# Three VectorE instructions fewer in the prologue of a one-token attention and MLP block

## The chip, the cores and the metric

The kernel runs on one core of a Trainium2 chip. The metric is the device time of one execution in microseconds. The kernel before took 191.74 us, the median of three runs (191.66 to 191.85).

The core's engines run side by side and meet at semaphores: TensorE (PE in the profile) multiplies matrices, VectorE (DVE) does elementwise work, reductions and 32x32 transposes, ScalarE (ACT) does functions such as exp and gelu, GpSimd (POOL) does general work, and SyncE (SP) issues most of the loads. Sixteen DMA engines move data between memory and the on-chip buffers. SBUF is the on-chip memory with 128 partitions, PSUM the accumulators that TensorE writes.

## The reference

One token passes through a layer norm, attention against a cache of 16384 keys and values with 32 query heads on 8 key heads, an output projection, and an MLP. In short:

```python
def _A_ref(x, k_cache, v_cache, wq, wo):
    q = (x @ wq).reshape(B, Sq, Hq, Dh).transpose(0, 2, 1, 3)
    k = jnp.repeat(k_cache, rep, axis=1)        # 8 key heads -> 32
    v = jnp.repeat(v_cache, rep, axis=1)
    scores = jnp.einsum("bhqd,bhkd->bhqk", q, k) * (Dh ** -0.5)
    p = _softmax(scores, axis=-1)
    o = jnp.einsum("bhqk,bhkd->bhqd", p, v)
    return o.transpose(0, 2, 1, 3).reshape(B, Sq, Hq * Dh) @ wo
...
x = A_x                                          # [1, 1, 512]
h = x + _A_ref(_layernorm(x), A_k_cache, A_v_cache, A_wq, A_wo)
h2 = h + _B_ref(_layernorm(h), B_w1, B_w2, B_w3, B_w4)
```

In `_B_ref` the shifted branch (`w1`, `w2`) is zero for a single token, since every shift moves the one row out; what is left is `gelu(layernorm(x) @ w3) @ w4` beside the residuals. The inputs are bf16: each of the two caches is 33.5 MB, wq and wo are 4.2 MB each, w3 and w4 1.8 MB each. Together that is the 79.17 MB that the profile counts as read.

## The kernel before, in words

The kernel is written as a list of operations with named tiles; a helper class turns reads and writes of the same name into semaphore waits. On each engine the instructions run in the order in which the program lists them. All large loads go through one queue, issued by SP in program order; a load waits until its target buffer is free.

There are three large buffers: `kb` (keys, two halves), `vb` (values) and `kt` (transposed keys). `wq` is loaded into `vb`, `wo` into the first half of `kb`, and `w3` and `w4` into the second half of `kb`, when these are free.

1. *Prologue* (lines 325 to 394). The token is loaded as four rows of 128 (`x4`). VectorE sets `mean4` and clears `ident_f`; GpSimd writes ones on its diagonal (line 332), which makes an fp32 unit matrix. Line 337 casts its top left 4x4 corner to bf16 (`ident`), line 338 spreads each of the four columns 32 times (`quarter`, 4 x 4 x 32). A matmul with `quarter` as weights (line 340) puts each of the four rows of the token on 32 partitions. A chain of small VectorE instructions computes the layer norm and ends in `xn` (line 346).
   Behind it VectorE sets constants: `nscale` (351), columns 2 and 3 of a scratch tile (352), two fields of zeros `zo` and `zd` of 128 x 224 fp32 (354, 355), and then masks made from `ident_f` (359 to 368). Two copies (370) put 32 columns of a mask into the middle of `zo` and `zd`; sliding a 128-column window over such a field places one pair's result in its own 32 rows (lines 436 and 464). GpSimd meanwhile clears `qb` and `pt` (356, 357). ScalarE loads its table for exp with a dummy instruction (353).
   Then TensorE multiplies `xn` with `wq` (381), and VectorE transposes and scatters the queries into `qb` (385, 391).
2. *Four pairs of key heads.* For each pair: VectorE transposes the keys in eight pieces for each half (400), TensorE computes scores (408), a short chain finds the maximum and takes exp on ScalarE (419 to 430), VectorE transposes the probabilities (434), TensorE multiplies with the values (447), and VectorE and TensorE gather the result (458 to 464). A key buffer is reloaded after its transposes, the value buffer after the products.
3. *End.* Output projection (506), second layer norm, the two MLP products (540, 568), sums (572, 574), and two small stores.

`spin` (line 263) issues matmuls whose results nobody reads.

Of the kernel before, what the change touches and what calls it, by code (L numbers as in the profile page):

```python
# [6 lines left out]
FP32 = mybir.dt.float32  # L7
BF16 = mybir.dt.bfloat16
# [124 lines left out]
def bass_sequential_preLN__gqa_block_cached__mixer_s_mlp__decode_kernel(  # L133
# [13 lines left out]
    with ExitStack() as ctx:  # L147
        sb = lambda name, shape, dt: ctx.enter_context(nc.sbuf_tensor(name, shape, dt))
# [15 lines left out]
        x4 = sb("x4", [4, 128], BF16)  # L164
        mean4 = sb("mean4", [128, 128], FP32)
        ident_f = sb("ident_f", [128, 128], FP32)
        ident = sb("ident", [4, 4], BF16)
        quarter = sb("quarter", [4, 4, 32], BF16)
        row32 = sb("row32", [128, 32], FP32)
        maskdd = sb("maskdd", [128, 4], FP32)  # L170
        maskgh = sb("maskgh", [128, 2, REP], FP32)
        rowgh = sb("rowgh", [128, 2, REP], FP32)
        rowc = sb("rowc", [128, 4], FP32)
        zo = sb("zo", [128, 224], FP32)
        zd = sb("zd", [128, 224], FP32)
        nscale = sb("nscale", [1, 128], FP32)
        scr = sb("scr", [128, 4], FP32)
        st = [sb(f"st{i}", [128, 16], FP32) for i in range(2)]
# [66 lines left out]
        def dve(fn, r=(), w=(), bank=()):  # L245
            return P.op("DVE", fn, r, w, bank)

        def act(fn, r=(), w=(), bank=()):
            return P.op("ACT", fn, r, w, bank)

        def pool(fn, r=(), w=(), bank=()):
            return P.op("POOL", fn, r, w, bank)

        def pe(fn, r=(), w=(), bank=()):
            return P.op("PE", fn, r, w, bank)

        def piece(cuts, m):
            return [lo <= m < hi for lo, hi in cuts].index(True)
# [49 lines left out]
        def inverse_root(i, n, by):  # L308
# [25 lines left out]
                                               channel_multiplier=1), r=["ident_f"], w=["ident_f"])  # L334


        dve(lambda e: e.tensor_copy(ident[:, :], ident_f[0:4, 0:4]), r=["ident_f"], w=["ident"])  # L337
        dve(lambda e: e.tensor_copy(quarter[:, :, :], ident[:, :].unsqueeze(2).to_broadcast([4, 4, 32])),  # L338
            r=["ident"], w=["quarter"])
        pe(lambda e: e.matmul(O_ps[0][:, 0:128], quarter[:, :, :].rearrange("p q u -> p (q u)"), x4[:, :],  # L340
                              start=True, stop=True), r=["quarter", "x4"], w=[("O", 0)], bank=[("O", 0)])
        row_sums(0, O_ps[0], ("O", 0))
# [5 lines left out]
            r=["hT", (("st", 0), 0), (("st", 0), 6)], w=["xn"])  # L348


        dve(lambda e: e.memset(nscale[:, :], -SCALE), w=["nscale"])
        dve(lambda e: e.memset(scr[:, 2:4], 0.0), w=["scr2"])
        act(lambda e: e.activation(scr[0:1, 0:1], mean4[0:1, 0:1], ACTF.Exp), r=["mean4"], w=["scr"])
        dve(lambda e: e.memset(zo[:, :], 0.0), w=["zo"])
        dve(lambda e: e.memset(zd[:, :], 0.0), w=["zd"])
        pool(lambda e: e.memset(qb[:, :, :, :], 0.0), w=["qb"])
        pool(lambda e: e.memset(pt[:, :, :, :, :], 0.0), w=["pt"])

# [1 line left out]
            r=["ident_f"], w=["row32"])  # L360
        dve(lambda e: e.tensor_reduce(maskdd[:, :], ident_f[:, :].rearrange("p (n d) -> p d n", d=4), AX.X, ALU.add),
            r=["ident_f"], w=["maskdd"])
# [14 lines left out]
        for j, (row, key) in enumerate(rows):  # L377
# [6 lines left out]
            for b in range(2):  # L384
# [3 lines left out]
                    r=[key], w=["qcol"], bank=[key])  # L388
# [103 lines left out]
        for n, (lo, hi) in enumerate(W4):  # L492
# [7 lines left out]
            r=["o_m"], w=["o_f"])  # L500
# [3 lines left out]
        for r_ in range(32):  # L504
# [3 lines left out]
               r=["o_b", ("r", 0, piece(WO, r_))], w=[("O", 0)], bank=[("O", 0)])  # L508
# [3 lines left out]
           r=["quarter", "x4"], w=[hkey], bank=[hkey])  # L512
# [7 lines left out]
        for q in range(4):  # L520
            pe(lambda e, q=q: e.matmul(h_ps[32 * q:32 * q + 32, 0:128], copies(row32[:, 0:1], 32),
                                       osum[:, q * 128:(q + 1) * 128], start=False, stop=True, skip_group_check=True),
               r=["osum", "row32"], w=[hkey], bank=[hkey])
# [3 lines left out]
        for i in range(2):  # L527
# [5 lines left out]
            r=["hT", (S, 0)], w=["hc"])  # L533
        act(lambda e: e.activation(hr2[64:128, :], h2_ps[64:128, 0:256], ACTF.Identity, bias=0.0, scale=1.0),
            r=["h2"], w=["hr2"], bank=["h2"])


        for k in range(NCH):
            for q in range(4):
                pe(lambda e, k=k, q=q: e.matmul(s_ps[32 * q:32 * q + 32, 0, 0:FQ], hc[:, k, :],  # L540
                                                w3_sb[:, k, q * FQ:(q + 1) * FQ], start=(k == 0), stop=(k == NCH - 1)),
                   r=["hc", ("r", 1, piece(W3, k))], w=[("s", 0)], bank=[("s", 0)])
# [7 lines left out]
        for n in range(2):  # L550
# [9 lines left out]
            r=["hr2", "xs2"], w=["xsum"])  # L560

        turns = {m: m % 2 if m < W4[0][1] else 0 for m in range(NHC)}
        for m in range(NHC):
# [3 lines left out]
            for o in range(2):  # L567
# [3 lines left out]
                   r=[("hcol", 2 * m // NHC), ("r", 1, 2 + piece(W4, m))], w=[key], bank=[("B" if t else "mn")])  # L571
        dve(lambda e: e.tensor_tensor(part[:, :], xsum[64:128, :], B_ps[64:128, 0:256], ALU.add),
            r=["B", "xsum"], w=["part"], bank=["B"])
        dve(lambda e: e.tensor_tensor(fin[:, :], part[:, :], n_ps[0:64, 0:256], ALU.add),  # L574
            r=["n", "part"], w=["fin"], bank=["mn"])
        for o, by in enumerate(("SP", "ACT")):
            P.op(by, lambda e, o=o: e.dma_start(out[0, 0:1, 256 * o:256 * o + 256], fin[32 * o:32 * o + 1, :]),
                 r=["fin"], w=[("out", o)], dma=f"out{o}")
# [32 lines left out]
```

## Time and profile before

| what | us |
|---|---|
| median of three runs | 191.74 |
| the profiled execution | 191.69 |
| its span, first to last instruction | 190.2 |
| TensorE busy in it | 116.7 (61%) |
| VectorE busy in it | 116.0 (61%) |
| ScalarE, GpSimd busy | 9.4, 7.0 |
| read from memory | 79.17 MB, 416 GB/s over the span |

In the rows that follow, `out<-in` names tiles, `x8` counts instructions, `L338` is a line of the kernel, and a bracket tells how long the engine had been idle before and what released it (`[5.81 <-DMA ...]`). `SPq` is SP's queue of DMA issues. Times are microseconds from the start of the span, unless a column is said to be in nanoseconds. In groups of instructions the numbers behind the bar are busy time, mean nanoseconds of one, and idle time before.

### The profile page before, as it was taken

How to read it: one execution, taken by the hardware profiler on the slowest of the kernel's cores; microseconds unless marked ns; L12 is line 12 of the kernel's file. 1: busy time of each engine (PE TensorE's matmuls, PEld its weight loads, DVE VectorE, ACT ScalarE, POOL GpSimd, SP SyncE). 2: the span in 40 equal slices, each digit the busy share in tenths (PEclk: the TensorE clock that was granted, in tenths of full speed). 3: DMA queues.
4: the chain of work that ended last, by engine and by line, in shares of the span. 5: the costliest groups of instructions: out<-in, count | busy, mean ns of one | idle time of the engine just before them, and what ended most of it. 6: DMA issues, size and time to landing. Idle time of an engine off the chain costs nothing.

```text
span 190.2 us, 1684 instructions
## 1 busy us (share of the span) xinstructions
PE 116.7 (61%) x700; PEld 43.7 (23%) x703; DVE 116.0 (61%) x179; ACT 9.4 (5%) x16; POOL 7.0 (4%) x15
## 2 busy tenths in 40 slices
PE   0128099893084004999447799935739896598673
PEld 0113034221031001422123222212213222233231
DVE  7756397983402007999452999844259897514274
ACT  3000000002000000000110000020000000500011
POOL 7100000000000000000000000000000000000032
PEclk9999858998559655899958999995796999669999
DMA  6999999999999999997999998999999999989992
GB/s 221 441 441 441 441 441 443 441 441 431 441 441 441 441 427 441 441 441 341 441 420 441 496 455 386 403 407 407 441 441 441 469 444 413 441 379 393 428 410 76
DMA packets 2610, 79.26 MB, mean 417 GB/s; under 512 B 298, under 2 KB 428, under 8 KB 556
## 3 DMA queue, kind: packets, MB, share of 16 engines
q1 hardware_dynamic: 2594, 79.17, 97.1%
q8 instruction: 5, 0.08, 0.2%
q14 instruction: 1, 0.01, 0.0%
q10 hardware_dynamic: 10, 0.00, 0.0%
HBM read 79.17 MB, written 0.00 MB: 416 GB/s over the span
## 4 chain that ended last, share of the span: by engine, by line
DMA 61%; DVE 31%; PE 4%; issue 1%; SPq 1%; ACT 1%; ACTq 0%
DMA kb<-in_A_k_cache_dram 47%; DVE kt L400 28%; DMA kb<-in_B_w_dram 15%; PE O_ps L447 3%; DVE pt L434 1%; SPq L226 1%; DVE mx L419 1%; ACT p_sb L430 1%; DVE od L461 1%; PE s_ps L408 1%; PE mn_ps L568 0%; DVE fin L574 0%; PE mn_ps L424 0%; PE mn_ps L420 0%; DVE od L458 0%
## 5 line engine op out<-in xcount | busy, mean ns | idle before, releaser
L408 PE MATMUL s_ps<-kt,qb 128*128 128x512 bf16 x256 | 69.3, 408 | 27.1 <-DVE kt L400 24.0
L400 DVE STREAM_TRANSPOSE kt<-kb 128x1024 int32<-128x1024 int32 x64 | 72.8, 1206 | 19.3 <-DMA kb<-in_A_k_cache_dram 19.3
L408 PEld LDWEIGHTS s_ps<-kt,qb 128*128 128x128 bf16 x256 | 22.4, 102 | 73.1 <-DVE kt L400 50.1
L447 PE MATMUL O_ps<-vb,pt 128*32 128x512 bf16 x256 | 20.0, 481 | 9.4 <-DMA vb<-in_A_v_cache_dram 7.4
L458 DVE TENSOR_SCALAR od<-O_ps,rowc 128x128 f32<-128x128 f32 x4 | 1.4, 351 | 26.3 <-PE O_ps L447 26.3
L434 DVE STREAM_TRANSPOSE pt<-p_sb 64x1024 bf16<-64x1024 bf16 x8 | 9.9, 1239 | 5.4 <-ACT p_sb L430 5.3
L447 PEld LDWEIGHTS O_ps<-vb,pt 128*32 128x32 bf16 x256 | 8.2, 117 | 20.3 <-issue 8.8
L430 ACT ACTIVATE p_sb<-s_ps,bias 128x1024 bf16<-128x1024 f32 x4 | 4.5, 1113 | 156.6 <-DVE nmh L426 156.6
L263 PE MATMUL O_ps<-kt,qb 128*128 128x512 bf16 x26 | 8.8, 478 | 0.6 <-issue 0.6
L419 DVE TENSOR_REDUCE mx<-s_ps 128x1 f32<-128x1024 f32 x4 | 4.9, 1224 | 4.5 <-PE s_ps L408 4.5
L381 PE MATMUL O_ps<-vb,xn 128*64 128x512 bf16 x16 | 3.2, 574 | 5.8 <-DMA vb<-in_A_wq_dram 5.8
L315 POOL TENSOR_SCALAR st<-st 128x1 f32<-128x1 f32 x1 | 0.2, 244 | 177.7 <-DVE st L300 177.7
L436 PE MATMUL A_ps<-acc,zd 128*128 128x1 f32 x8 | 2.1, 337 | 6.3 <-ACT p_sb L430 6.3
L464 PE MATMUL A_ps<-od,zo 128*128 128x128 f32 x8 | 2.0, 326 | 5.5 <-DVE od L461 5.5
L420 PE MATMUL mn_ps<-ident_f,mx 128*1 128x128 f32 x8 | 1.5, 271 | 5.3 <-DVE mx L419 5.3
L461 DVE SCALAR_TENSOR_TENSOR od<-O_ps,rowc,od 128x128 f32<-128x128 f32 x12 | 4.2, 351 | 0.4
L263 PEld LDWEIGHTS O_ps<-kt,qb 128*128 128x128 bf16 x29 | 3.1, 121 | 4.8 <-issue 3.7
L337 DVE CAST ident<-ident_f 4x4 bf16<-4x4 f32 x1 | 3.8, 3849 | 0.6 <-POOL ident_f L332 0.6
L340 PE MATMUL O_ps<-x,quarter 4*128 4x128 bf16 x1 | 0.3, 281 | 5.8 <-DVE quarter L338 5.8
L385 DVE STREAM_TRANSPOSE qcol<-O_ps 128x256 f32<-128x256 f32 x4 | 1.6, 428 | 3.4 <-PE O_ps L381 3.4
L436 PEld LDWEIGHTS A_ps<-acc,zd 128*128 128x128 f32 x8 | 1.8, 281 | 6.6 <-ACT p_sb L430 6.6
L506 PE MATMUL O_ps<-kb,o_b 128*32 128x512 bf16 x32 | 2.1, 381 | 1.6 <-DMA kb<-in_A_wo_dram 1.6
(90 smaller groups left out, 49.3 us busy)
## 6 DMA issues: line engine op xcount, KB each, us to landing
kb<-in_A_k_cache_dram SPq DMA_DIRECT2D x6, 4096.0 KB, 24.0
vb<-in_A_wq_dram SPq DMA_DIRECT2D x1, 4096.0 KB, 12.4
kb<-in_A_wo_dram SPq DMA_DIRECT2D x1, 3072.0 KB, 27.2
kb<-in_B_w_dram SPq DMA_DIRECT2D x1, 1792.0 KB, 24.4
kb<-in_B_w_dram SPq DMA_DIRECT2D x1, 1280.0 KB, 27.1
kb<-in_A_wo_dram SPq DMA_DIRECT2D x1, 1024.0 KB, 29.3
kb<-in_B_w_dram SPq DMA_DIRECT2D x1, 384.0 KB, 27.6
kb<-in_B_w_dram SPq DMA_DIRECT2D x1, 128.0 KB, 27.5
```

The costliest lines, as they stand in the source:

```text
L263: pe(lambda e: e.matmul(O_ps[out][:, :], qb[:, 0, 0, 0:128], kt[:, 0:512], start=True, stop=True), r=["qb", ("kt", 0)], w=[("O", out)], ba ...
L337: dve(lambda e: e.tensor_copy(ident[:, :], ident_f[0:4, 0:4]), r=["ident_f"], w=["ident"])
L381: pe(lambda e, row=row, k=k, g=g, at=at: e.matmul(row[64 * g:64 * g + 64, :], copies(xn[:, k:k + 1], 64), wq_sb[:, at:at + REP * DH], star ...
L400: dve(lambda e, view=view: e.transpose(view(kt), view(kb[y])), r=[("r", y, n) for n in range(RPARTS)], w=[("kt", t)])
L408: pe(lambda e, n=n, c=c: e.matmul(s_ps[:, y, :], qb[:, n, j, QPAD - 4 * c:QW - 4 * c], ktv[:, n // 2, n % 2, :, 8 * c:8 * c + 8, :], start ...
L419: dve(lambda e: e.tensor_reduce(mx[:, :], s_all, AX.X, ALU.max), r=[("s", 0), ("s", 1)], w=["mx"], **both)
L430: act(lambda e: e.activation(p_sb[:, :], s_all, ACTF.Exp, bias=bias[:, 0:1], scale=float(SCALE), accum_out=acc[:, :]), r=[("s", 0), ("s", ...
L434: dve(lambda e, g=g: e.transpose(pt[64 * g:64 * g + 64, :, :, g, :], p_sb[64 * g:64 * g + 64, :]), r=["p"], w=["pt"])
L436: pe(lambda e: e.matmul(A_ps[:, 128:129], zd[:, 96 - 32 * j:224 - 32 * j], acc[:, :], start=(j == 0), stop=(j == PAIRS - 1), skip_group_ch ...
L447: pe(lambda e, q=q, ct=ct, xl=xl, ch=ch: e.matmul(O_ps[j % 2][32 * ct:32 * ct + 32, :], pt[:, xl, ch, :, :].rearrange("p g u -> p (g u)"), ...
L461: dve(lambda e, block=block, c=c: e.scalar_tensor_tensor(od[:, :], block, rowc[:, c:c + 1], od[:, :], ALU.mult, ALU.add), r=[key, "rowc", ...
L506: pe(lambda e, r_=r_, q=q: e.matmul(O_ps[0][32 * q:32 * q + 32, :], copies(o_b[:, r_:r_ + 1], 32), wo_sb[:, r_ * D:(r_ + 1) * D], start=(r ...
```

## The change

`ident` disappears: `quarter` is made by one VectorE instruction that reads the 4x4 corner of the fp32 unit matrix, spreads it and casts it to bf16. `zo` and `zd` become the two halves of one tile `zz` with one memset for both. The memset of columns 2 and 3 of `scr` is dropped. Values and the order of everything else stay.

```diff
-        ident = sb("ident", [4, 4], BF16)
         quarter = sb("quarter", [4, 4, 32], BF16)
...
-        zo = sb("zo", [128, 224], FP32)
-        zd = sb("zd", [128, 224], FP32)
+        zz = sb("zz", [128, 2, 224], FP32)
+        zo, zd = zz[:, 0, :], zz[:, 1, :]
...
-        dve(lambda e: e.tensor_copy(ident[:, :], ident_f[0:4, 0:4]), r=["ident_f"], w=["ident"])
-        dve(lambda e: e.tensor_copy(quarter[:, :, :], ident[:, :].unsqueeze(2).to_broadcast([4, 4, 32])),
-            r=["ident"], w=["quarter"])
+        dve(lambda e: e.tensor_copy(quarter[:, :, :], ident_f[0:4, 0:4].unsqueeze(2).to_broadcast([4, 4, 32])),
+            r=["ident_f"], w=["quarter"])
...
         dve(lambda e: e.memset(nscale[:, :], -SCALE), w=["nscale"])
-        dve(lambda e: e.memset(scr[:, 2:4], 0.0), w=["scr2"])
         act(lambda e: e.activation(scr[0:1, 0:1], mean4[0:1, 0:1], ACTF.Exp), r=["mean4"], w=["scr"])
-        dve(lambda e: e.memset(zo[:, :], 0.0), w=["zo"])
-        dve(lambda e: e.memset(zd[:, :], 0.0), w=["zd"])
+        dve(lambda e: e.memset(zz[:, :, :], 0.0), w=["zo", "zd"])
```

## The prediction

> **What bounds the kernel now.** I read the profile page's slices of the span first, to see which resource is never idle.
>
> ```profile
> DMA  6999999999999999997999998999999999989992
> GB/s 221 441 441 441 441 441 443 441 441 431 441 441 441 441 427 441 441 441 341 441 420 441 496 455 386 403 407 407 441 441 441 469 444 413 441 379 393 428 410 76
> ...
> q1 hardware_dynamic: 2594, 79.17, 97.1%
> ```
>
> From the second slice to the last but one the 16 DMA engines are busy nine tenths of the time or nearly; the one queue that carries all loads took 97.1% of the engines' span. The whole run is one stream of 79.17 MB. Next the chain that ended last, in order of time (start, length, what).
>
> ```profile
> 1.64 31.51 DMA kb<-in_A_k_cache_dram
> ...
> 33.17 9.14 DVE kt L400 x8
> ...
> 42.36 30.09 DMA kb<-in_A_k_cache_dram
> ...
> 123.06 26.99 DMA kb<-in_A_k_cache_dram
> ...
> 160.12 27.61 DMA kb<-in_B_w_dram
> 187.74 0.04 issue
> 187.78 0.64 PE mn_ps L568 x8
> 188.43 0.02 issue
> 188.45 0.41 DVE fin L574
> ```
>
> The chain passes through VectorE's transposes of keys (L400), because a load waits for its buffer to come free. That is not a stall of the stream: the load joins a queue that still has work. The issue times of SP's queue and one landing show the margin.
>
> ```profile
> 18.26 0.33 SPq L226 DMA_DIRECT2D vb<-in_A_v_cache_dram  x1
> 42.36 0.33 SPq L226 DMA_DIRECT2D kb<-in_A_k_cache_dram  x1
> 58.67 0.33 SPq L226 DMA_DIRECT2D vb<-in_A_v_cache_dram  x1
> ...
> 136.71 0.33 SPq L226 DMA_DIRECT2D vb<-in_A_v_cache_dram  x1
> ...
> 159.27 1.75 SPq L226 DMA_DIRECT2D kb<-in_B_w_dram  x4
> ```
> ```profile
> 53.13 5.44 PE L447 MATMUL O_ps<-vb,pt 128*32 128x512 bf16 x64 [5.13 <-DMA vb<-in_A_v_cache_dram]
> ```
>
> The first value load is issued at 18.26, while the second half of the first keys is in flight until 1.64 + 31.51 = 33.15: 14.9 us to spare. The keys of pair 1 are issued at 42.36; the values ahead of them land at 53.13, where TensorE stops waiting for them: 10.8 us to spare. The second value load goes out at 58.67 with keys landing until 42.36 + 30.09 = 72.45, 13.8 us; the fourth at 136.71 with keys landing until 150.05, 13.3 us. Compute that moves by less than some 10 us therefore cannot open a gap in the stream. The run is: start of the stream, bytes over rate, and the tail behind the last landing (187.74 to 190.2).
>
> **The change part by part.** All of it lies in the first 13 us. Its rows, from the timeline (start, length, engine, line, operation):
>
> ```profile
> 1.36 0.29 POOL L332 TENSOR_SCALAR_AFFINE_SELECT ident_f<-ident_f 128x128 f32<-128x128 f32 x1 [0.94 <-DVE ident_f L331]
> 1.60 2.18 POOL L356 MEMSET qb<- 128x2496 bf16 x1
> 1.69 3.85 DVE L337 CAST ident<-ident_f 4x4 bf16<-4x4 f32 x1 [0.57 <-POOL ident_f L332]
> ...
> 3.72 1.80 POOL L357 MEMSET pt<- 128x2048 bf16 x1
> 5.57 0.21 DVE L338 COPY quarter<-ident 4x128 bf16<-4x128 bf16 x1
> ...
> 5.84 0.28 PE L340 MATMUL O_ps<-x,quarter 4*128 4x128 bf16 x1 [5.84 <-DVE quarter L338]
> ...
> 10.25 0.29 DVE L346 TENSOR_SCALAR xn<-hT,st 128x4 bf16<-128x4 f32 x1
> ...
> 10.60 0.06 DVE L352 MEMSET scr<- 128x2 f32 x1
> 10.66 0.24 DVE L354 MEMSET zo<- 128x224 f32 x1
> 10.90 0.24 DVE L355 MEMSET zd<- 128x224 f32 x1
> 11.07 0.23 DVE L359 TENSOR_REDUCE row<-ident_f 128x32 f32<-128x128 f32 x1
> ...
> 12.11 0.17 DVE L370 COPY zd<-maskgh 128x32 f32<-128x32 f32 x1
> ...
> 13.24 3.20 PE L381 MATMUL O_ps<-vb,xn 128*64 128x512 bf16 x16 [5.81 <-DMA vb<-in_A_wq_dram]
> ...
> 15.20 0.78 DVE L385 STREAM_TRANSPOSE qcol<-O_ps 128x256 f32<-128x256 f32 x2 [2.91 <-PE O_ps L381]
> ...
> 22.85 3.50 DVE L400 STREAM_TRANSPOSE kt<-kb 128x1024 int32<-128x1024 int32 x3 [2.97 <-DMA kb<-in_A_k_cache_dram]
> ```
>
> *The selector.* A 4x4 cast is charged 3.85 us. It starts at 1.69, inside GpSimd's clear of qb (1.60 to 3.78), and ends at 5.54, 0.02 after GpSimd's clear of pt (3.72 + 1.80 = 5.52): nearly all of it is waiting on GpSimd, not work. The change drops this cast and turns L338 into a cast from ident_f, so the wait is inherited, not removed, if the new cast behaves like the old one. Then quarter is ready between 5.54 (the 128 elements cost no more behind the wait than the 16 did) and 5.78 (a full 0.21 behind it, as now). I take 5.6: 112 elements more at 0.83 ns (the memset rows below: 80 ns for 96) are 0.09 us behind 5.54. That is 0.2 us earlier, with 0 and 0.24 as ends. The other case: it does not wait, starts at 1.69 and takes the 0.21 of L338, so it ends near 1.9. The chain behind it down to xn (10.25 + 0.29 = 10.54) would then come up to 3.9 us earlier, near 6.7.
>
> The Trainium skill (SBUF — State Buffer, "Who interferes with whom") says that a VectorE copy or cast in a two-port mode and a GpSimd instruction exclude each other for whole instructions. The row above agrees: 3.85 us for sixteen elements, ending with the second clear. By that rule the new cast waits too and xn comes near 10.3; by the other case it would come near 6.7, and TensorE would wait for wq in both.
>
> *The scr memset.* Columns 2 and 3 of scr are read by nobody (L353 and L484 write columns 0 and 1). Its pitch in the rows is 10.66 - 10.60 = 0.06 us, saved.
>
> *One memset for two.* The two take 11.07 - 10.66 = 0.41 us of VectorE's time. The rows for memset by size:
>
> ```profile
> L354 DVE MEMSET zo<- 128x224 f32 x1 | 0.2, 245 | 0.0
> ...
> L330 DVE MEMSET mean<- 128x128 f32 x1 | 0.2, 165 | 0.8 <-PEq L596 0.8
> ```
>
> 96 elements more cost 80 ns, so 448 elements cost 245 + 224 x 80 / 96 = 432 ns. The next instruction started 0.07 before the old one had ended (10.90 + 0.245 against 11.07), so the pitch would be some 0.36: 0.05 us saved, between 0 and 0.07. The later writers of zo and zd (L370) and readers (L436, L464) have the same two names to wait for; the first reader runs after 33 us, far behind.
>
> *Sum on VectorE:* 0.2 + 0.06 + 0.05 = 0.31 us before the end of its setup, 12.11 + 0.17 = 12.28, which becomes about 11.97; xn, ahead of both memsets, gains only the 0.2. Neither was late. TensorE's first use of xn starts at 13.24 and waited 5.81 us for wq, the load's landing:
>
> ```profile
> vb<-in_A_wq_dram SPq DMA_DIRECT2D x1, 4096.0 KB, 12.4
> ```
>
> (issued at 0.72, so about 13.1). xn has 13.24 - 10.54 = 2.7 us of cover; VectorE itself then sits idle 2.91 us before L385 and 2.97 us before the first key transpose. All 0.31 us goes into these idle stretches. If that cover were gone (a faster wq load), xn's 0.2 would show behind it, but the end would still hang on the stream. No DMA, no ScalarE and no GpSimd instruction moves. So the sum on the path is 0.
>
> *Addresses.* One thing reaches beyond the prologue. The program lays its tiles out one behind the other in slots of 32 bytes; ident took one slot ahead of everything from quarter on. zz has the size of zo and zd together. So kb, vb and kt all begin 32 bytes lower: kb at byte 51904 of each partition instead of 51936, vb at 117440 instead of 117472. In the old layout these starts are odd multiples of 32, in the new one multiples of 64. Every packet of the stream has its target moved. No row shows such a packet at the other phase. A bound: the values at 53.13 and the 8.39 MB of keys behind them at 72.45 give 8.39 / 19.32 = 434 GB/s. All 79.17 MB at that rate would be 182.4 us, against 187.74 - 1.7 = 186.0 in which they moved. If the whole 3.6 us were a cost of bad starts and went away, 188.1 would result; if as much came on top, 195.3. These ends are far apart; the 434 GB/s row, which has the same packets and sizes, is nearest, and I take 0.
>
> **The rivals.** (a) *The prologue is on the path after all*: VectorE's 0.31 us shows, 191.4 by the profiled execution. For it: the stream's second load needs TensorE's L381 done, which needs xn. Against it: 2.7 us of cover there and 14.9 us behind. Where the time does move a little for this reason, it is less than a measurement can tell.
>
> (b) *Packets become cheaper* by starting on a rounder address. There are 2594 / 16 = 162 packets for each DMA engine, so 1 ns per packet is 0.16 us. Removing more than 2.4 ns per packet gives less than 191.3; the whole 3.6 us above is 22 ns per packet, but the stream's slow start and its uneven end are in that too. The uneven end is seen in the windows (us, then busy time by engine, granted clock, DMA share, GB/s):
>
> ```profile
> 185.00:187.80 2.80, 1.64 (x27) 0.69 (x25) 1.77 (x5) 0.85 (x2) 1.35 (x4) 1.00 0.51 197
> ```
>
> Half of the last 2.8 us of DMA time is empty, 1.4 us of the 3.6, so at most 2.2 us, 14 ns per packet, is left for starts. Likely size 1 to 8 ns: 190.4 to 191.5.
> The Trainium skill (DMA: Bandwidth & Descriptors, "How a descriptor splits into AXI transactions") says that transactions begin on multiples of 256 bytes and that bytes in front of an unaligned start still cost beats of 32 bytes. If it holds for the target side, the start moves from 224 to 192 past a multiple, one beat fewer; at the page's 850 MHz, an estimate of 1.2 ns per packet, 0.19 us, 191.5. No row shows it.
>
> (c) *Packets become dearer*, the case on the other side: the same 162 packets per engine, each with a costlier write at the new start. It decides the result from 2.4 ns per packet on (192.1); with half of the 14 ns on top it is 1.1 us, 192.8. For it: only that nothing shows the new phase. Against it: a start that divides by 64 instead of 32 has no reason to cost more.
>
> (d) *The new cast keeps GpSimd out* instead of waiting. The clears of qb and pt would end later by the length of one cast, 0.2 us. qb is next written at 19.02 (L391), 13 us after. Nothing follows.
>
> **How the numbers follow.** The profiled execution took 191.69 us (span 190.2 and 1.49 around it), 0.05 under the median of the three runs, 191.74. Sum 0 on the path: 191.7. The runs lie within 191.66 to 191.85; a change under 0.2%, 0.38 us, can hardly be told from none. Chances: no visible change 0.73 (with the small end of b, and d, inside it); (a) beyond 0.38 us 0.02; (b) beyond it 0.14; (c) beyond it 0.11. So faster 0.16, same 0.73, slower 0.11. The range 191.2 to 192.2 holds the forecast's own part and the nearer halves of (b) and (c); the ends 188.1 and 195.3 belong to cases that I hold for less than 1 in 20 each.
>
> **What the profile after would show.** Right: no row for L337's cast, one cast onto quarter that ends near 5.6 with GpSimd's second clear; one memset of 128x448 near 430 ns; TensorE's first L381 still at 13.2 behind wq; VectorE's idle time before L385 up from 2.91 to about 3.2; the last landing within 0.3 us of 187.74; 441 GB/s in the same slices. The cast step is wrong if quarter's cast ends near 2; xn then comes near 6.7 and the end stays. The forecast is wrong if the last landing moves by more than 0.4 us with the issue times' margins unchanged (then the packets' price moved: b or c), or if TensorE's first L381 moves with xn (a).

## The result and the profile after

In the first comparison, eleven executions of each kernel, the changed kernel took 191.39 us (191.14 to 191.62) against 191.91 (191.56 to 193.04): a ratio of 0.9967, 95% interval 0.9953 to 0.9982. In a second one it took 191.72 against 191.78, ratio 0.9996, interval 0.9972 to 1.0021. The profiled execution took 191.42 us, with a span of 190.1 and 1.32 around it (before: 191.69, 190.2 and 1.49).

In some executions of most kernels here TensorE's mean granted clock is lower and the span up to 1.9 us longer (a trace of one is shown under *What was not expected*); these executions count in the ratios, so the spans compared below, and the times around them, are medians of the executions whose mean granted clock is 0.84 or more.

The slices of the page after (the columns are those of the page before):

```profile
DMA  6999999999999999997999999989999999989991
GB/s 242 428 434 441 441 441 443 441 441 431 441 441 441 441 428 441 441 441 341 441 441 434 483 441 431 428 379 393 434 434 441 469 431 441 441 371 400 428 405 69
...
q1 hardware_dynamic: 2594, 79.17, 97.0%
```

The stream of loads fills the run as before, with as many packets and as many bytes. The prologue, from the timeline after (start, length, engine, line, operation):

```profile
1.61 2.18 POOL L352 MEMSET qb<- 128x2496 bf16 x1
3.73 1.80 POOL L353 MEMSET pt<- 128x2048 bf16 x1
```
```profile
1.70 3.90 DVE L336 CAST quarter<-ident_f 4x128 bf16<-4x128 f32 x1 [0.58 <-POOL ident_f L331]
...
10.07 0.29 DVE L344 TENSOR_SCALAR xn<-hT,st 128x4 bf16<-128x4 f32 x1
10.31 0.17 DVE L349 MEMSET nscale<- 1x128 f32 x1
10.52 0.43 DVE L351 MEMSET zz<- 128x448 f32 x1
10.88 0.23 DVE L355 TENSOR_REDUCE row<-ident_f 128x32 f32<-128x128 f32 x1
...
11.92 0.18 DVE L366 COPY zz<-maskgh 128x32 f32<-128x32 f32 x1
15.10 0.78 DVE L381 STREAM_TRANSPOSE qcol<-O_ps 128x256 f32<-128x256 f32 x2 [3.00 <-PE O_ps L377]
```
```profile
13.14 3.62 PE L377 MATMUL O_ps<-vb,xn 128*64 128x512 bf16 x16 [5.89 <-DMA vb<-in_A_wq_dram]
```

The cast onto quarter inherited the wait for GpSimd and ended at 1.70 + 3.90 = 5.60, behind the clear of pt (3.73 + 1.80 = 5.53). The one memset took 0.43 us. VectorE's setup ended at 12.10 instead of 12.28, and TensorE began at 13.14 as soon as wq was there: still the load that it waited for, 5.89 us long. The end of the chain:

```profile
1.62 31.41 DMA kb<-in_A_k_cache_dram
...
42.25 29.93 DMA kb<-in_A_k_cache_dram
...
159.88 27.74 DMA kb<-in_B_w_dram
187.61 0.04 issue
187.66 0.64 PE mn_ps L564 x8
188.32 0.41 DVE fin L570
```

The second half of the first keys lands at 33.03 instead of 33.15, the last load at 187.61 instead of 187.74. Of the 0.27 us between the two profiled executions 0.13 lie in the stream and the rest around the span. One issue time of SP's queue moved the other way, from 18.26 to 19.75:

```profile
19.75 0.33 SPq L225 DMA_DIRECT2D vb<-in_A_v_cache_dram  x1
```
```profile
16.53 3.13 PE L377 MATMUL s_ps<-vb,xn 128*64 128x512 bf16 x16
```

The second half of the product with wq took 3.13 us here and 1.91 in the kernel before. This does not go with the instructions removed: of the kernels below, the instructions alone issue this load at 18.08, and the kernel before with 288 bytes of pad issues it at 19.61. The load still has 33.03 - 19.75 = 13.3 us to spare.

### The profile page after: what moved, and what is told of

It is laid out like the page before. It is cut to its first block, busy times and chain, and to the rows that moved or that the text cites. A ratio compares the mean times of both kernels' runs of the same rounds, so it can differ in the third digit from the quotient of the medians.

```text
span 190.1 us, 1681 instructions
## 1 busy us (share of the span) xinstructions
PE 118.2 (62%) x700; PEld 44.2 (23%) x703; DVE 115.8 (61%) x176; ACT 9.4 (5%) x16; POOL 7.0 (4%) x15
## 3 DMA queue, kind: packets, MB, share of 16 engines
q1 hardware_dynamic: 2594, 79.17, 97.0%
## 4 chain that ended last, share of the span: by engine, by line
DMA 61%; DVE 31%; PE 4%; issue 1%; SPq 1%; ACT 1%; ACTq 0%
DMA kb<-in_A_k_cache_dram 46%; DVE kt L396 28%; DMA kb<-in_B_w_dram 15%; PE O_ps L443 3%; DVE pt L430 1%; SPq L225 1%; DVE mx L415 1%; ACT p_sb L426 1%; DVE od L457 1%; PE s_ps L404 1%; PE mn_ps L564 0%; DVE fin L570 0%; PE mn_ps L420 0%; PE mn_ps L416 0%; DVE od L454 0%
## 5 line engine op out<-in xcount | busy, mean ns | idle before, releaser
L432 PE MATMUL A_ps<-acc,zz 128*128 128x1 f32 x8 | 2.1, 337 | 6.3 <-ACT p_sb L426 6.3
L460 PE MATMUL A_ps<-od,zz 128*128 128x128 f32 x8 | 2.0, 326 | 5.5 <-DVE od L457 5.5
L336 DVE CAST quarter<-ident_f 4x128 bf16<-4x128 f32 x1 | 3.9, 3905 | 0.6 <-POOL ident_f L331 0.6
L432 PEld LDWEIGHTS A_ps<-acc,zz 128*128 128x128 f32 x8 | 1.8, 280 | 6.6 <-ACT p_sb L426 6.6
```

The lines of the kernel that those rows point to most:

```text
L336: dve(lambda e: e.tensor_copy(quarter[:, :, :], ident_f[0:4, 0:4].unsqueeze(2).to_broadcast([4, 4, 32])), r=["ident_f"], w=["quarter"])
L432: pe(lambda e: e.matmul(A_ps[:, 128:129], zd[:, 96 - 32 * j:224 - 32 * j], acc[:, :], start=(j == 0), stop=(j == PAIRS - 1), skip_group_ch ...
```

## The experiments

Two things had changed at once: VectorE's program is three instructions shorter, and the large buffers begin 32 bytes lower. The first four kernels separate them. Theory A puts the gain on the address, theory I on the instructions, theory N on scatter.

**The instructions alone.** The changed kernel, with ident's place in memory kept:

```diff
         ident_f = sb("ident_f", [128, 128], FP32)
+        sb("slot", [4, 4], BF16)
         quarter = sb("quarter", [4, 4, 32], BF16)
```

> The changed kernel with an unused 4x4 bf16 tile kept in ident's place, so that every tile behind it lies where it lay before: kb at byte 51936 of each partition. Theory A (the targets' address): the gain of 0.3% is gone, 191.9 us against 191.9 before (within 0.3), and a packet of 64 KB takes its old median of 2421 ns. Theory I (the three VectorE instructions): the gain stays, 191.4. Theory N (no real difference, the two kernels' runs scattered): this run lies anywhere between 191.4 and 191.9 and so does the next.

Measured: 191.53 us against 191.79, ratio 1.0 (0.998 to 1.002). Span 190.2 as before; the time around it 1.32 us (1.27 to 1.37) as in the changed kernel, where the kernel before has 1.54 (1.37 to 1.69). The packets are those of before: a 64 KB packet has its median at 2421 ns. So the span's gain is gone with the old addresses, and a part of 0.22 us that lies outside the span stays. None of the three theories had a gain in two parts.

**The addresses alone.** The kernel before, with ident's place moved behind the large buffers:

```diff
-        ident = sb("ident", [4, 4], BF16)
         quarter = sb("quarter", [4, 4, 32], BF16)
...
         kt = sb("kt", [128, 128 * DH], BF16)
+        ident = sb("ident", [4, 4], BF16)
```

> The kernel before with all its instructions, only that ident's place in memory is behind the large buffers, so that kb begins at byte 51904 as in the changed kernel. Theory A: the gain is here, 191.4 to 191.7 us, and every packet's median falls by about 1 ns (64 KB: 2421 to 2420 ns); 162 packets per DMA engine make that 0.2 us. Theory I: as before, 191.9, and the packets unchanged or changed without an effect on the end. Theory N: anywhere between.

Measured: 191.74 against 191.79, ratio 1.0019 (0.9993 to 1.0045); in half of these twelve executions the mean granted clock is below 0.84. In the others the span is 190.0 (189.9 to 190.1), 0.2 below the kernel before, and 1.55 us lie around it as before. The 64 KB packets fell to 2420 ns. The complement of the run above: the span's part belongs to the addresses, the part around it does not.

**How far the address reaches.** The kernel before, with unused bytes ahead of kb: 288, so that the large buffers start at a multiple of 512, and 64, so that they start 32 bytes past a multiple of 256.

```diff
+        sb("pad", [128, 144], BF16)        # the second kernel: [128, 32]
         kb_all = sb("kb", [128, 256 * DH], BF16)
```

> The kernel before with 288 unused bytes ahead of kb: kb, vb and kt begin at a multiple of 512 bytes (52224), 224 bytes past a multiple of 256 before. Theory A with a grid of 256 bytes: seven steps of 32 bytes fewer ahead of the first full piece of a packet; if one step is the 1 ns by which the packets of the changed kernel fell, 7 to 8 ns less per packet (64 KB: 2413 ns), 162 packets, 1.1 to 1.3 us, 190.6 to 190.8. Theory A with a grid of 64 bytes: no more than the changed kernel has, 191.4 to 191.7. Theories I and N: 191.9, packets at 2421 ns.

> The kernel before with 64 unused bytes ahead of kb: the three buffers begin 32 bytes past a multiple of 256 (52000), an odd multiple of 32 as before. Theory A with a grid of 256: one step of 32 bytes above the run that starts at a multiple, six below the kernel before: 1.0 to 1.2 us less than before, 190.7 to 190.9, a 64 KB packet 1 ns above that run's. Theory A with a grid of 64: as before, 191.9, since 32 is as odd as 224. Theories I and N: 191.9.

Measured: 191.18 against 191.79 at a multiple of 512, ratio 0.9962 (0.9943 to 0.9981), span 189.5; 191.85 at 32 past a multiple of 256, ratio 0.9994 (0.9977 to 1.0012), span 190.35. The chain's end in the first of the two:

```profile
1.63 31.38 DMA kb<-in_A_k_cache_dram
...
159.74 27.23 DMA kb<-in_B_w_dram
186.97 0.04 issue
187.01 0.63 PE mn_ps L569 x8
187.67 0.41 DVE fin L575
```

The last load lands 0.77 us earlier than before. One more start, on a multiple of 256 that is none of 512, has 32 unused bytes ahead of kb:

```diff
+        sb("pad", [128, 16], BF16)
         kb_all = sb("kb", [128, 256 * DH], BF16)
```

> The kernel before with 32 unused bytes ahead of kb: the large buffers begin at 51968, a multiple of 256 but not of 512. If a packet is undisturbed from a multiple of 256 on: span 189.5 us and packets as in the run that starts at a multiple of 512 (24 KB: 912 ns in all). If it takes 512: span 190.0 to 190.2, 24 KB packets up to 922 ns.

Measured: 191.13 against 191.78, ratio 0.9965 (0.9941 to 0.9988), span 189.4. From the packets' records of the traces, the 128 packets of 24 KB (the first part of wo), with the start of the target past a multiple of 256; the last column adds up the times of all packets of the queue of loads and divides by 16 engines:

```
start   kernel                      ns, 10% / median / 90%   span us   last landing us   all packets, us per engine
 224    before                      914 / 915 / 922          190.2     187.74            184.70
 192    changed                     913 / 914 / 921          190.1     187.61            184.41
  32    before, 64 bytes of pad     914 / 915 / 922          190.35    187.99            184.67
   0    before, 32 bytes (256)      912 / 912 / 912          189.4     186.92            184.28
   0    before, 288 bytes (512)     912 / 912 / 912          189.5     186.97            184.30
```

At a multiple of 256 the spread of the packets is gone, and 512 gives no more. 32 past costs as much as 224 past, so the price does not grow by steps of 32 bytes: that form of theory A fell with this run. The mean of the 24 KB packets falls from 916.7 to 912.0 ns. That is not the gain of every packet: a 64 KB packet gains 3 ns in the median (2421 to 2418), one of 32 KB none (1213 in both), and one of 4 bytes, of which there are 289 among the 2594, none either. Added up, the packets take 0.40 us per engine less at a multiple of 512 than in the kernel before. The last landing moved by 0.77, and the spans of the two kernels that start at a multiple of 256 are shorter by 0.7 to 0.8. So about half of the gain is time of the packets themselves; the rest lies between and around them, goes with the same starts, and is not explained here.

For the changed kernel's start the sum settles more than a single landing. In the seven traces that start at 192 it is 184.41 to 184.58 us per engine, in the four that start at 224 or 32 it is 184.63 to 184.70: the two sets do not overlap, and their means differ by 0.16 us. The last landing of the changed kernel moved by 0.13.

**Both together.** The changed kernel with 320 unused bytes ahead of kb, a multiple of 512:

```diff
+        sb("pad", [128, 160], BF16)
         kb_all = sb("kb", [128, 256 * DH], BF16)
```

> The changed kernel with 320 unused bytes ahead of kb, so that the three large buffers begin at a multiple of 512. If the two gains are separate (the span shorter by the packets' price, the time around the span shorter with the three instructions gone), both add: span 189.5 us as in the run with the pad alone, 1.32 around it as in the changed kernel, 190.8. If they are one gain seen twice, no better than either: 191.1 to 191.4.

Measured: 190.68 against 191.84, ratio 0.9934 (0.9911 to 0.9957); span 189.3, 1.33 around it. The two gains add, and this version's median is the lowest of all kernels here.

**The length of VectorE's program.** The changed kernel with one, two or three memsets more, into an unused tile behind the large buffers:

```diff
         kt = sb("kt", [128, 128 * DH], BF16)
+        dz = sb("dz", [128, 8], FP32)
...
         dve(lambda e: e.memset(nscale[:, :], -SCALE), w=["nscale"])
+        for i in range(3):                    # or 2, or 1
+            dve(lambda e, i=i: e.memset(dz[:, 2 * i:2 * i + 2], 0.0), w=[("dz", i)])
```

> The changed kernel with three more VectorE memsets of 128x2 into an unused tile behind the large buffers: as many VectorE instructions as before, addresses as changed. If the length of VectorE's program sets the time around the span: 1.54 us around it again, span as in the changed kernel, 190.06: 191.6. If it is not the number but one of the three removed instructions: 1.32, 191.4.

> The same with two more memsets, one VectorE instruction fewer than before. If the time around the span grows by a fixed part for each instruction (0.22 us over three): 1.47 us around it, 191.53. If it is a step, at some length of the program at which one more piece of it is fetched: 1.32 or 1.54, nothing between, 191.4 or 191.6.

> The changed kernel with one more VectorE memset of 128x2 into the unused tile, two VectorE instructions fewer than before. The run with two more had 1.59 us around its span, so a fixed part for each instruction has fallen. If the time around the span is a step: 1.32 (step between one and two more: 191.4) or 1.55 (step between none and one: 191.6), and the fetch of 8 KB of instructions behind the last instruction is in the trace in the second case alone.

Measured: 191.73, ratio 1.0006 (0.998 to 1.0033), with three; 191.85, 1.0008 (0.9985 to 1.0031), with two; 191.48, 1.0002 (0.9984 to 1.0021), with one. The time around the span, as medians over executions:

```
VectorE instructions against the kernel before   around the span, us
as many (before; three back)                     1.54; 1.49
one fewer (two back)                             1.59
two fewer (one back)                             1.41
three fewer (changed, twice; instructions alone;
             both together; cast first)          1.32, 1.30; 1.32; 1.33; 1.29
```

It follows the number of VectorE instructions, not which ones: three memsets of another tile bring it back. It is not a fixed part for each, since one fewer gives nothing. The packets' records show an 8 KB fetch of instructions that starts 1.2 to 1.6 us behind the span's end in the traces of all kernels with as many or one fewer, and in none with two or three fewer. That is a step between one and two fewer, as that theory wanted; but the 1.41 in between fits neither of its two numbers. Nor do the times fit a wait for this fetch: it ends 1.7 to 1.9 us behind the span, while no more than 1.7 us was measured around the span in all, ahead of it and behind it, and 1.49 in the profiled execution of the kernel before, where the fetch ends at 1.73. So the connection with the number of VectorE instructions is shown, the fetch is a companion whose part is not shown, and the 0.09 us between two and three fewer stay open. Whether the other engines' programs count in the same way was not tried.

**The cover of the prologue, from both sides.** In the kernel before, the memset of scr gave way to a memset of kt ahead of the variance, with as many instructions and the same addresses:

```diff
         row_sums(0, O_ps[0], ("O", 0))
+        dve(lambda e: e.memset(kt[:, 0:6144], 0.0), w=[("kt", t) for t in range(3)])
         variance(0)
...
-        dve(lambda e: e.memset(scr[:, 2:4], 0.0), w=["scr2"])
```

> The kernel before with the memset of scr taken out and a memset of kt's first 6144 columns put in ahead of the variance, as many instructions and the same addresses: VectorE clears for some 6.4 us (0.83 to 1.04 ns per element), so xn comes near 17 us, 3.7 us behind wq's landing, where it was 2.7 us ahead of it. If the prologue is covered by the stream of loads: 191.75 as before, L381 starts near 17, the last landing stays at 187.6. If the prologue is on the path once its cover is gone: 195.

Measured: 191.70 us against 191.84, ratio 0.9978 (0.9957 to 1.0). Three rows of the timeline (one of TensorE) and two of the chain:

```profile
8.22 2.62 DVE L343 MEMSET kt<- 128x3072 uint32 x1 [0.59 <-issue]
...
13.22 0.29 DVE L347 TENSOR_SCALAR xn<-hT,st 128x4 bf16<-128x4 f32 x1
```
```profile
13.56 3.63 PE L381 MATMUL O_ps<-vb,xn 128*64 128x512 bf16 x16 [6.12 <-DVE xn L347]
```
```profile
160.20 27.49 DMA kb<-in_B_w_dram
187.69 0.04 issue
```

The clear made xn 3.0 us later, less than half of what was expected, since it ran as 3072 words and took 2.62 us. It was still enough to use up the cover: TensorE now waits for xn and not for wq, and begins 0.32 us later than in the kernel before. The last landing stayed at 187.69 (before 187.74). From the other side, the changed kernel with GpSimd's clear held back until quarter is there:

```diff
-        pool(lambda e: e.memset(qb[:, :, :, :], 0.0), w=["qb"])
+        pool(lambda e: e.memset(qb[:, :, :, :], 0.0), r=["quarter"], w=["qb"])
```

> The changed kernel with GpSimd's clear of qb waiting for quarter, so that the cast onto quarter runs with GpSimd idle. If the 3.9 us of the cast are a wait for GpSimd: it takes 0.2 us, quarter is ready near 2.0, xn near 6.7 instead of 10.3, qb cleared near 4.3; the last landing and the time stay (191.4), since wq still lands at 13. If the cast is slow by itself: it ends at 5.6 again and GpSimd's clears come 4 us later.

Measured: 191.38 us against 191.78, ratio 0.9985 (0.9964 to 1.0006).

```profile
1.70 0.21 DVE L336 CAST quarter<-ident_f 4x128 bf16<-4x128 f32 x1 [0.57 <-POOL ident_f L331]
1.97 2.18 POOL L352 MEMSET qb<- 128x2496 bf16 x1 [0.31 <-DVE quarter L336]
...
6.87 0.29 DVE L344 TENSOR_SCALAR xn<-hT,st 128x4 bf16<-128x4 f32 x1
...
13.04 1.49 PE L377 MATMUL O_ps<-vb,xn 128*64 128x512 bf16 x6 [8.97 <-DMA vb<-in_A_wq_dram]
```

The cast takes 0.21 us when GpSimd is idle: the other 3.69 were a wait. xn is ready at 7.16 instead of 10.36, and TensorE waits longer for wq. The span is 190.0 us in this run and 190.1 in the changed kernel without it. xn moved from 7.2 to 13.5 over these kernels, TensorE's start from 13.04 to 13.56, and the end followed neither.

**The changed kernel again**, beside these:

> The changed kernel beside the others and the kernel before on one chip. By the two terms found (0.17 us of span from the addresses, 0.22 us around it from the shorter VectorE program) 191.35 to 191.45 against 191.75, a ratio of 0.998. If the first comparison's 0.9967 was more than these two: 191.1.

Measured: 191.72 against 191.78, ratio 0.9996 (0.9972 to 1.0021). The executions with a clock of 0.84 or more have 191.54, span 190.2 (190.1 to 190.6), 1.30 around it; the 24 KB packets again 913 / 914 / 921 ns. The time around the span repeats closely, the span only within its scatter.

## Why the prediction was right, and where it was not

*The prologue.* Right in its numbers and its consequence. The cast onto quarter waited for GpSimd and ended at 5.60 (forecast 5.6); the 128x448 memset took 430 ns (forecast 432); xn came at 10.36 (forecast near 10.3); TensorE began at 13.14 behind wq. VectorE's setup ended 0.18 us earlier, not 0.31: the large memset began 0.21 us behind nscale (10.31 to 10.52), where scr's and then zo's had begun 0.11 and 0.17 behind it, so of the 0.06 and the 0.05 almost nothing was left. The idle time before the first transpose grew to 3.00 us, not 3.2, for this reason and because wq came 0.1 us earlier. That none of this reaches the end is shown from both sides by the runs in which xn came 3 us later and 3 us earlier. The later one delays TensorE by 0.32 us, which is the size of rival (a): it is refuted for that size, not for larger ones. One sign came only in part: 441 GB/s stands in 18 slices and not in the 20 of before, 15 of them the same.

*Weighing the rule on GpSimd.* The choice between 10.3 and 6.7 for xn fell on the right side: the cast onto quarter takes 3.90 us beside GpSimd's clears and 0.21 with GpSimd held back. The Trainium skill (SBUF — State Buffer, "Who interferes with whom") says that a VectorE cast in a two-port mode and a GpSimd instruction exclude each other for whole instructions, and this pair of runs agrees; in which mode the cast ran no row tells.

*The addresses.* The step "I take 0" was mis-sized. The term was there: 0.16 us per engine over all packets, about 1 ns for each, and its sign was that of rival (b), whose lower end it just reaches; rival (c) is refuted for this start. That 1 ns per packet makes 0.16 us held as an average, but not packet by packet, since the price differs by size. The whole price of an uneven start, 0.7 to 0.8 us of span, was less than the 2.2 that the prediction left room for. The runs show a grid of 256 bytes: 24 KB packets take 912 ns without spread from a multiple of 256 on. The Trainium skill (DMA: Bandwidth & Descriptors, "How a descriptor splits into AXI transactions") has a grid of 256 bytes too; its count of beats, carried over to the target side, does not hold, since 32 past a multiple of 256 cost as much as 224 past and not one seventh. That rival (b)'s estimate by that count, 0.19 us, came near the measured 0.16 is therefore luck.

*The term that was not there.* The sum was made on the span and took the 1.49 us around it as fixed. The medians fell from 1.54 to 1.32, the larger half of the gain; the prediction had no term for it, and no rival.

*The sum.* 0 was forecast. The two terms are about 0.15 and 0.22 us, together 0.37, 0.19%, just short of what the prediction called visible. The first comparison gave 0.33% (0.18 to 0.47), the second 0.04% (from 0.28% faster to 0.21% slower): the two terms lie in both intervals, in the first one barely. Its medians differ by 0.52 us, and the 0.15 beyond the two terms did not come again. 191.39 us is inside the range. "No visible change" was right in what it said of VectorE's work and a little short of the truth of the whole. That the two terms it left out were small was luck: no row that it used had their size.

## What to carry to other kernels

In this kernel, one stream of loads from end to end, shorter compute in a covered stage was worth nothing to the span, but the same edit moved the stream's targets: see where the large buffers begin. Here a pad that put them on a multiple of 256 bytes was worth 0.35 to 0.38%, more than the three instructions removed. A sum made on the span leaves out what lies around it; compare an execution's time with its span before and after.

## What was not expected of the hardware

- A packet's time depends on where its target starts: 24 KB took 912 ns in all but a few packets from a multiple of 256 bytes on, and mostly 913 to 922 at 32, 192 or 224 past one.
- The time around the span depends on the number of VectorE instructions: 1.32 us with three fewer, 1.54 with the old number.
- A slow last stage. In the address-only run, and in those with one and three memsets back, the profile caught an execution with the granted clock at half, 0.50 from 185.0 to 187.8 us (the address-only one in windows: us, then busy time by engine, granted clock, DMA share, GB/s). The kernel before, whose row for 185.0 to 187.8 stands in the prediction, and then the address-only kernel:

```profile
187.80:190.30 2.50, 0.61 (x8) 0.29 (x8) 0.71 (x2) 0.00 (x0) 0.00 (x0) 0.93 0.00 0
```
```profile
185.00:187.80 2.80, 2.80 (x20) 0.90 (x13) 1.10 (x4) 0.85 (x2) 1.43 (x4) 0.50 0.42 161
187.80:190.30 2.50, 1.89 (x30) 0.84 (x28) 1.45 (x4) 0.00 (x0) 0.00 (x0) 0.87 0.00 0
```

The loads end no later there, but TensorE is busy all through the first stretch and still has 30 matmuls for the second; its span is 191.6 us. Part of what it does then is `spin`, whose results nobody reads (the kernel before, then the address-only kernel):

```profile
184.65 1.25 PE L263 MATMUL O_ps<-kt,qb 128*128 128x512 bf16 x5
```
```profile
186.30 2.29 PE L263 MATMUL O_ps<-kt,qb 128*128 128x512 bf16 x5
```

In the kernel before, these five end 1.0 us ahead of the next matmuls' inputs; at the half clock they end at 188.59 and the last matmuls follow at once, so the end hangs on TensorE and not on the stream. What decides in which executions the clock drops was not tried, nor was a kernel without these five.
